# Moving one chunk's scores, its weighting and its normalisation ahead of weight roundings in the front of an mLSTM + FFN kernel

## The chip, the cores and the metric

The kernel runs on one core of a Trainium2 chip. The metric is the device time of one execution in microseconds. Before the change the median of three runs is 489.75 us (489.66 to 490.23).

## What is computed

Two stages follow each other. The first is an mLSTM cell over `q`, `k`, `v` of shape (4, 8, 768, 40) with an input, a forget and an output gate:

```python
for t in range(S):
    m_new = max(f[t] + m, i[t])
    f_stab, i_stab = exp(f[t] + m - m_new), exp(i[t] - m_new)
    C = f_stab * C + i_stab * outer(v[t], k[t])
    n = f_stab * n + i_stab * k[t]
    y[t] = sigmoid(o[t]) * (C @ q[t]) / max(abs(n @ q[t]), 1)
```

Its output is turned into `x` of shape (3072, 320), and the second stage is a feed-forward block with a squared ReLU:

```python
h = maximum(x @ w_in, 0)      # w_in: 320 x 2048
out = (h * h) @ w_out         # w_out: 2048 x 320
```

The weights arrive as 64-bit numbers and are made into f32 on the chip.

## The kernel before

**Tiles.** The sequence is cut into 24 chunks of 128 tokens (batch 0 has chunks 0 to 5). For a chunk `s` the recurrence is computed in its parallel form: `transposes` turns k and q, `scores` multiplies them (L595), `weigh` makes the decay weights W on ScalarE (ACT) from a log-decay tile `A_bc`, after `mask` on GpSimd (POOL) has cut it to the causal part, and `weighted` multiplies scores and W into P on VectorE (DVE, L609). `rows_begin` and `rows_end` (L700) then multiply old state, P and k with the values on TensorE (PE); between their two halves stands a DVE instruction of one element, the marker (L737), that reads the first half's result and writes a spare place that the second half's operand tile holds, so that PE's second half waits for it. `normalise` (L910 to L921) makes the chunk's rows of `x_sb`, and `turn_rows` (L951, L953) turns them into `xT`.

**Groups.** Two chunks make a group of 256 tokens. The first feed-forward product of a group is done in four parts of 512 columns. `ffn1_main` (L977) multiplies the first 256 rows of `w_in` in two K halves `a` of 128 rows, `ffn1_rest` (L988) adds the last 64 rows. `relu_half` (L1001) moves the result from PSUM to SBUF, `square_half` (L1007) squares it.

**Weight roundings.** The 64-bit weights come in 18 pieces. `Rounding.fetch` (L206) issues the load of a piece on SyncE's queue (SP), `words` (L216, L218) does two ACT passes, `join` three DVE passes (L227, L231, L232) and one addition on POOL (L236), and then fetches another piece into the buffer that it has freed. Pieces 0 to 9 are `w_in`: 0, 1 and 2 serve FFN1 part 0; 3 and 4 part 1; 5, 6 and 7 part 2; 8 and 9 part 3. Raw pieces 3, 7 and 11 lie in a tile that is lent (`lent_t`), the others in three buffers in turn.

**Order.** Nothing reorders the program: each engine and each DMA queue runs its instructions in the order in which the Python code issues them. The front is a hand-written order: chunks 0 and 1, then a loop over eight steps `u`, two for each of the chunks 2 to 5. An even step has scores, `weighted` and the next chunk's `weigh`; an odd step has the products with values, the next transposes and a normalisation. Every step has one part of FFN1 and one or more roundings, up to the count in `NEXT`. `idle(n)` (L1224) issues n matmuls of zeros whose result nobody reads. After the front, from about 86 us on, the other 18 chunks run beside the second product of the groups, with PE busy nearly throughout.

The change touches the loop nest of `ffn1_main` and steps `u` = 0, 1 and 2.

## Time and profile before

| | before |
|---|---|
| median of the runs | 489.75 us (489.66 to 490.23) |
| profiled execution | 489.91 us, span 488.2 us, mean granted clock 0.992 |
| PE busy | 476.6 us (98%) |
| weight loads busy | 444.6 us (91%) |
| DVE, ACT, POOL busy | 344.1, 244.0, 224.9 us |
| DMA | 69.93 MB, 143 GB/s mean |

The page tells busy time by engine, the span in forty slices, the queues, the chain of work that ended last, and groups of instructions. PE is busy 98% of the span, so its idle time (11.6 us in all) and the clock that it is granted are what a change in the front can work on. The front is about 86 us long; in it DMA is near its full share, and every engine works for several purposes in turn, so a wait there is best read from the timeline of each queue.

### The profile page before, as it was taken

What the parts mean: (1) busy time and instruction counts of PE and PEld (TensorE: products, weight loads), DVE (VectorE), ACT (ScalarE), POOL (GpSimd) and SP (SyncE); (2) the same over time, 40 slices, a digit from 0 to 9 for tenths busy, and PEclk for the clock granted to TensorE, in tenths of its full rate; (3) what the DMA queues carried; (4) which work ended last, traced back from release to release, by engine and by line L of the source; (5) the groups of instructions that cost most, each with busy time, mean ns of one, the idle gap of its engine ahead of it and who ended that gap; (6) DMA issues with size and microseconds to landing.
All of it is one profiled execution on the core that took longest, in us unless ns stands there. A gap on an engine that the chain in (4) does not pass through costs nothing.

```text
span 488.2 us, 15700 instructions
## 1 busy us (share of the span) xinstructions
PE 476.6 (98%) x6389; PEld 444.6 (91%) x6389; DVE 344.1 (70%) x725; ACT 244.0 (50%) x534; POOL 224.9 (46%) x337
## 2 busy tenths in 40 slices
PE   9989999999898999999999999999999999999997
PEld 5877788779798999999999999999999999999997
DVE  7959768888886974775876975965965957635441
ACT  4697897644641651652752751653653651514300
POOL 5454545567881876826746836734833111020000
PEclk9988999999999999999999999999999999999999
DMA  8999998779997698677677686696773322200000
GB/s 174 209 253 265 259 202 209 201 144 230 194 190 108 165 169 164 164 155 155 149 149 153 159 165 145 155 155 128 156 144 87 93 58 82 55 15 15 1 28 27
DMA packets 192839, 69.93 MB, mean 143 GB/s; under 512 B 158144, under 2 KB 181504, under 8 KB 192768
## 3 DMA queue, kind: packets, MB, share of 16 engines
q1 hardware_dynamic: 157424, 56.39, 51.7%
q0 software_dynamic: 6080, 10.16, 9.4%
q10 hardware_dynamic: 29264, 2.39, 4.7%
q8 instruction: 50, 0.82, 0.7%
q14 instruction: 21, 0.17, 0.1%
HBM read 55.69 MB, written 18.92 MB: 153 GB/s over the span
## 4 chain that ended last, share of the span: by engine, by line
PE 77%; DMA 10%; SPq 6%; DVE 3%; ACT 1%; issue 1%; POOL 0%; DVEq 0%; ACTq 0%; POOLq 0%
PE h_ps L1061 32%; PE h_ps L1140 22%; PE h_ps L1173 7%; PE h_ps L977 5%; DMA kqT<-kq_rows 3%; PE numT L823 3%; DMA kq<-in_q_dram 2%; PE numT L801 2%; SPq L399 2%; PE tp L587 1%; PE h_ps L988 1%; DMA xT<-x_rows 1%; PE numT L835 1%; DMA raw<-in_moe_w_in_dram 1%; SPq L206 1%
## 5 line engine op out<-in xcount | busy, mean ns | idle before, releaser
L1061 PE MATMUL h_ps<-T,S 128*128 128x160 f32 x352 | 51.6, 300 | 0.7 <-DVE S L1056 0.7
L1061 PEld LDWEIGHTS h_ps<-T,S 128*128 128x128 f32 x352 | 48.9, 190 | 1.1 <-PE h_ps L1061 0.9
L1061 PE MATMUL h_ps<-w_out,g 128*128 128x160 f32 x336 | 48.8, 302 | 0.0
L1061 PEld LDWEIGHTS h_ps<-w_out,g 128*128 128x128 f32 x336 | 46.2, 190 | 1.1 <-issue 0.5
L1077 DVE TENSOR_TENSOR y_sb<-y_sb,h_ps 128x160 f32<-128x160 f32 x44 | 14.0, 318 | 45.2 <-PE h_ps L1061 45.1
L1154 ACT COPY r_sb<-h_ps 128x512 f32<-128x512 f32 x20 | 11.7, 584 | 65.5 <-PE h_ps L1140 54.0
L1140 PE MATMUL h_ps<-xT,w_in 128*128 128x128 f32 x320 | 43.2, 278 | 0.0
L1140 PE MATMUL h_ps<-lent_t,w_in 128*128 128x128 f32 x320 | 42.3, 275 | 0.0
L1173 PE MATMUL h_ps<-xT,w_in 64*64 64x128 f32 x960 | 39.5, 272 | 1.8 <-DVE r_sb L1156 1.8
L1132 POOL TENSOR_TENSOR lent_t<-xT 128x128 f32<-128x128 f32 (+1 forms) x18 | 10.3, 592 | 66.7 <-DVE xT L943 50.6
L1140 PEld LDWEIGHTS h_ps<-xT,w_in 128*128 128x128 f32 x320 | 39.2, 192 | 1.6 <-issue 1.2
L375 POOL DMA_DIRECT2D va<-in_v_dram x64 | 39.3, 630 | 0.3 <-issue 0.3
L1140 PE MATMUL h_ps<-lent_t 128*128 128x128 f32 x320 | 39.1, 275 | 0.0
L1140 PEld LDWEIGHTS h_ps<-lent_t,w_in 128*128 128x128 f32 x320 | 39.0, 192 | 0.0
L1140 PEld LDWEIGHTS h_ps<-lent_t 128*128 128x128 f32 x320 | 37.3, 192 | 0.2 <-issue 0.2
L1173 PEld LDWEIGHTS h_ps<-xT,w_in 64*64 64x64 f32 x960 | 35.1, 133 | 2.6 <-DVE r_sb L1156 2.1
L510 ACT ACTIVATE A_bc<-A_bc,b_R 128x64 f32<-128x64 f32 (+1 forms) x128 | 35.6, 362 | 0.1
L1191 ACT ACTIVATE g<-h_ps 128x512 f32<-128x512 f32 x12 | 7.2, 597 | 53.6 <-PE h_ps L1140 36.3
L479 POOL TENSOR_SCALAR_AFFINE_SELECT A_bc<-A_bc 64x512 f32<-64x512 f32 x32 | 25.7, 802 | 17.0 <-ACT kq L497 15.8
L977 PE MATMUL h_ps<-xT,w_in 128*128 128x256 f32 x128 | 31.6, 402 | 0.0
L858 DVE STREAM_TRANSPOSE tn<-numT 128x256 f32<-128x256 f32 x36 | 14.0, 425 | 23.4 <-PE numT L801 15.5
L531 POOL TENSOR_TENSOR vw<-va,A_bc 128x328 f32<-128x328 f32 x13 | 11.5, 886 | 39.6 <-ACT A_bc L510 39.6
(231 smaller groups left out, 1213.5 us busy)
## 6 DMA issues: line engine op xcount, KB each, us to landing
A_bc<-a_slots SPq DMA_DIRECT2D x32, 256.0 KB, 4.3
kq<-num_rows SPq DMA_DIRECT2D x80, 64.0 KB, 3.1
num_rows<-tn SPq DMA_DIRECT2D x18, 256.0 KB, 2.4
raw<-in_moe_w_out_dram SPq DMA_DIRECT2D x7, 640.0 KB, 4.8
og<-in_o_gate_dram SPq DMA_DIRECT2D x24, 160.0 KB, 5.1
x_rows<-x_sb SPq DMA_DIRECT2D x20, 192.0 KB, 2.6
xT<-x_rows SPq DMA_DIRECT2D x80, 48.0 KB, 2.6
out_dram<-y_sb SPq DMA_DIRECT2D x23, 160.0 KB, 2.5
```

Source lines behind the costliest of these rows:

```text
L375: eng.dma_start(dst[HALVES[n], PR * (1 - late_keys) : PR * (2 - late_keys)], src[HALVES[late_keys], PR * m : PR * (m + 1)],)
L479: nc.gpsimd.affine_select(part, part, compare_op=ALU.is_ge, fill=-1e30, base=0, pattern=[[0, PR], [0, 2], [1, DP]], channel_multiplier=-1,)
L510: nc.scalar.activation(A[0][:, x, to], A[0][:, x, to], AF.Exp, bias=b_R[:, b, c, own, x : x + 1],)
L531: nc.gpsimd.tensor_tensor(d["vw"][:].rearrange("p (own x) d -> p own x d", own=2), d["va"][:].rearrange("p (own x) d -> p own x d", own=2) ...
L823: nc.tensor.matmul(d["numT"][m][DP * e : DP * e + wide, i, t0:], lhsT=va_w[s % NKQ][keys, at * D1 : at * D1 + wide], rhs=rhs, start=(s % N ...
L858: nc.vector.transpose(to[:, 2 * m : 2 * m + 2], d["numT"][m].rearrange("p c t -> p (c t)"))
L977: nc.tensor.matmul(hs[i][:, n, :], lhsT=w_in[:, a, fb * P : (fb + 1) * P], rhs=xT[:, :, a, :], start=(n == 0 and a == 0), stop=False,)
L1061: nc.tensor.matmul(to, lhsT=lhsT[:, p], rhs=rhs[:, p, :], start=(start and p == 0), stop=(p == NPAIR - 1), skip_group_check=True,)
L1077: add = lambda to, a, b: nc.vector.tensor_tensor(to, a, b, op=ALU.add)
L1140: nc.tensor.matmul(to[:, n, :], lhsT=lhsT[:, 4 * q + n, :], rhs=rhs, start=(start and n == 0), stop=True, skip_group_check=True,)
L1154: nc.scalar.copy(m1[:], X[:])
L1173: nc.tensor.matmul(to[cols, n, :], lhsT=w_in2[rows, 4 * q + n, cols], rhs=rhs, start=(start and n == 0), stop=True, skip_group_check=True,)
```

## The change

In `ffn1_main` the loop over the two K halves goes outside, so that all four column blocks are multiplied with the first 128 rows of the weights before any is multiplied with the second 128.

In the front, join 3 (which stood ahead of the loop) and join 4 (in step 0) each move behind something:

- step 0: the scores of chunk 2 go between FFN1 part 0's main and rest; the mask of chunk 3 follows at once, then P of chunk 2, and only then join 3. Step 0 ends with four joins done instead of five.
- step 1: join 4 stands between the two halves of chunk 2's products, behind the marker. The load of `A_bc` for chunk 4 is thereby issued ahead of raw piece 8. The normalisation of chunk 2 goes ahead of join 5, and the tanh of chunk 3's output gate behind the copies of the turned k and q.
- step 2: `idle(3)` becomes `idle(1)`.

Nothing is computed otherwise than before.

```diff
-        for i in range(2):
-            for n in range(2):
-                fb = 4 * pp + 2 * n + i
-                for a in range(2):
+        for a in range(2):
+            for i in range(2):
+                for n in range(2):
+                    fb = 4 * pp + 2 * n + i
                     nc.tensor.matmul(
                         hs[i][:, n, :], lhsT=w_in[:, a, fb * P : (fb + 1) * P], rhs=xT[:, :, a, :],
                         start=(n == 0 and a == 0), stop=False,
...
     weigh(2, masked=True)
     decay_old(2)
     rounding.words()
-    rounding.join()
-    NEXT = (5, 8, 10, 11, 12, 13, 14, 16)
+    NEXT = (4, 8, 10, 11, 12, 13, 14, 16)
...
             if u == 0:
-                ffn1(0, 0)
+                ffn1_main(0, 0)
                 scores(2)
+                ffn1_rest(0, 0, st["half"][0])
+                mask(3)
             else:
                 if u == 2:
-                    idle(3)
+                    idle(1)
...
             weighted(s)
             if u == 0:
-                mask(s + 1)
-                rounding.step()
+                rounding.join()
+                rounding.words()
+                rounding.words()
...
             if u == 1:
                 half_tanh(2)
-                half_tanh(3)
...
                 (rows_begin if s < X_SQ else attend_begin)(s)
+                if u == 1:
+                    rounding.join()
                 copies = transposes(s + 1, (True, True))
                 (rows_end if s < X_SQ else attend_end)(s)
...
+            if u == 1:
+                normalise(s)
             if u != 3:
                 rounding.join(fetch=u < 7)
             if u == 1:
                 load(4)
                 values(s + 1)
-            if s < X_SQ:
+            elif s < X_SQ:
                 normalise(s)
...
             copies()
+            if u == 1:
+                half_tanh(3)
             rounding.words()
             ffn1(u // 4, u % 4)
```

## The prediction

> **What bounds the kernel.** I read the page's first two parts, then the waits of TensorE (PE), the windows around the one dip of its clock, the chain, and last the queues' timelines from 20 to 60 us, where the change lies.

> ```profile
> PE 476.6 (98%) x6389; PEld 444.6 (91%) x6389; DVE 344.1 (70%) x725; ACT 244.0 (50%) x534; POOL 224.9 (46%) x337
> ...
> PEclk9988999999999999999999999999999999999999
> ...
> PE numT L700 <- DVE g_c L609: 0.7, 1, 0.7
> PE tp L555 <- DMA kq<-in_q_dram: 0.7, 1, 0.7
> ...
> 29.90:33.31 3.41, 2.48 (x80) 1.94 (x76) 3.31 (x6) 2.56 (x7) 2.51 (x2) 1.00 1.01 229
> 33.31:36.73 3.42, 2.95 (x45) 2.54 (x46) 1.13 (x4) 3.42 (x11) 1.26 (x1) 0.50 0.69 122
> 36.73:40.14 3.41, 3.41 (x9) 2.69 (x9) 3.31 (x9) 2.66 (x6) 1.98 (x3) 0.50 0.98 228
> 40.14:43.56 3.42, 3.42 (x20) 2.24 (x20) 3.25 (x8) 1.82 (x4) 1.02 (x2) 1.00 1.00 362
> ...
> 132.30:135.72 3.42, 2.16 (x94) 2.01 (x98) 2.98 (x6) 3.00 (x5) 1.49 (x3) 1.00 1.07 245
> ...
> 23.31 10.43 DMA kq<-in_q_dram
> 33.73 0.04 issue
> 33.78 1.12 PE tp L555 x4
> ...
> 42.95 0.76 PE idle L1224 x3
> ```

> PE is the bound, so only three things in the front can be won: two gaps (0.73 us until P of chunk 2, 0.67 us until q of chunk 3 lands), the filler L1224 (0.76 us), and the half clock from 33.31 to 40.14. In the windows the columns behind the length are busy us of PE, its weight loads, DVE, ACT, POOL, then granted clock, DMA share and GB/s. The clock falls at the end of a stretch that holds both gaps and only small matmuls, and stays low for 6.83 us. The chain says why PE starts again at 33.78: q's DMA, issued at 23.31 and 10.43 us under way.

> ```profile
> 41.16 0.68 ACT L216 ACTIVATE mag<-lent_t 128x512 f32<-128x512 f32 x1 [1.42 <-POOL vw L537]
> 42.98 1.08 ACT L1001 ACTIVATE g<-h_ps 128x512 f32<-128x512 f32 x2 [0.57 <-PE h_ps L988]
> 44.35 0.48 ACT L956 COPY xT<-tp 128x384 f32<-128x384 f32 x1 [0.28 <-PE tp L953]
> ...
> 52.12 0.16 DVE L737 TENSOR_SCALAR kq<-numT 1x1 f32<-1x1 f32 x1
> 52.36 0.33 PEld L700 LDWEIGHTS numT<-vw,kq 64*64 64x64 f32 x16 [0.17 <-DVE kq L737]
> ```

> Here ACT is seen to be the second bound: its second rounding of piece 7 starts at 41.16, when that piece's DMA lands (issued 35.65, 5.4 us), and everything after it is in one file, up to DVE's marker L737, for which PE waits at 52.36.

> **Part by part.** The profiled execution took 489.91 us (span 488.2, 1.7 around it); the median of the runs is 489.75. Differences below are worked out in the span and then taken from the median.

> 1. *Scores of chunk 2 ahead of the 64-row rest of FFN1.* The same 16 records of L595 (1.06 us) and 8 of L988 (1.14) swap places, so PE reaches 30.0 us as before. P (L609, 1.29 for both halves) needs the scores at 29.1 instead of 30.06, and as DVE no longer does a rounding (28.35 to 30.25) before it, it runs 29.1 to 30.4 instead of 30.28 to 31.57. The 0.73 us gap goes.

> 2. *What is late next.* PE does L700 (some 1.2 us) and the four k transposes from 30.0 and is done at about 31.9 (k lands at 22.77 + 8.6 = 31.4) instead of 33.11. Then it waits for q. Nothing ahead of q on SP is moved, so q lands at 33.73 as before, and the gap there is 1.8 us instead of 0.67. Gain of parts 1 and 2 together: 0.

> 3. *The clock.* The stretch 29.90 to 33.31 holds the same work after the change: 72 records of L700 and 4 transposes, with at most 0.1 us of L988 in place of the scores' end, and 1.4 us idle at its end instead of 0.96 in two pieces. PE's busy time alone does not decide: the stretch 132.30 to 135.72 has less (2.16) and keeps the clock. Weighing every record by the part of the array it fills (rows x columns / 128 x 128) times its columns streamed, twice for f32, I get 2254 for the stretch that loses the clock and 2860 for the one at 132.30 that keeps it. After the change I get 2254 to 2480. The next stretch (q's transposes, 40 records, two of FFN1) is unchanged too. So the clock falls at 33.31 and returns at 40.14: 0. Bounds: -3.4 us (half of 6.83) if it stays up and nothing else binds; +1.7 if a third stretch of 3.41 us is lost.

> [...]

> 4. *P, mask and marker ahead of roundings.* POOL's mask of chunk 3 (1.28) goes ahead of the rounding's addition; A_bc lands at 21.99 + 8.5 = 30.5, so it runs to 31.8 instead of 32.94, and ACT's exponentials (2.45) start after the relu at 32.1 instead of 32.97. Nobody waits for them: DVE needs them at 46. Join 3 moves to 30.4-32.3 (1.9), the marker to 32.3, join 4 (2.45) to 32.5-35.0, its addition to 36.3 on POOL. PE's rest of chunk 2 starts at 34.83 after q's transposes, as before. FFN1 part 1 starts at 36.28 and needs piece 4 only for its second half, 3.6 us later at half clock. Cost 0, hidden under q's DMA; uncovered, the addition would cost 0.1.

> 5. *K halves.* 16 records of L977 per part (3.72) in another order, none added. The second piece is needed 1.9 us later, the second bank 0.9 us earlier; the relus that free it (1.08) end 0.8 us or more ahead, part 3 excepted (point 8). From 0.3 gain (piece 9 is added until 53.51, part 3 starts at 53.20) to 0.2 loss; taken: 0.

> 6. *Normalisation ahead of join 5.* x_sb is ready at about 40 instead of 42.30. Join 5 (1.85) ends at 41.7 instead of 39.05; POOL's addition and vw of chunk 3 move from 39.20-41.16 to 41.7-43.7. Part 2 needs piece 5 at 44.8: hidden by 1.8 us.

> 7. *Filler.* Two of three L1224 go: 0.76 x 2/3 = 0.51 us. PE reaches the turned rows at 43.2 instead of 43.71, with x_sb long ready. Of this, ACT passes on less: its relu starts at 42.98 as before (PE's L988 ends at 42.95), the copy of xT at 44.06 instead of 44.35. From there piece 8, the exponentials, piece 9, join 9 and the marker follow on ACT and DVE without a break, so marker and PE stand at 52.07 instead of 52.36. Gain 0.29 us. Between 0.29 and 0.51 I take 0.3, since PE does wait for that marker.

> 8. *SP's queue.* A_bc of chunk 4 goes ahead of raw 8 (0.8 us each way, landing at 42.4 and 43.4, needed from 44). Raw 9 needs the buffer that join 5 frees, so it is issued at 41.75 instead of 39.12, and k, q and v of chunk 4 and raw 10 stand behind it. Issued at once after it, q lands at about 48 (was 39.98 + 7.2 = 47.2), and PE transposes it at 51. Raw 10 lands near 51 instead of 50.1, and ACT wants it at 50.5: piece 10 and the relu of part 2 may be 0.5 to 1 us late, which part 3 feels by 0 to 0.2 and ACT's idle 1.55 us before 58.02 takes up. SP stood idle 46.74-49.26, so it has caught up by raw 12. Cost 0 to 0.2; taken 0, as rows with idle follow.

> From 53 us PE, DVE, ACT and SP are all 0.3 us earlier, so the later chains move as a whole. Sum: 0 + 0 + 0 - 0.3, so 489.75 - 0.3 = **489.5 us** rounded.

> **Rivals.**

> *The clock stays up.* If the stretch counts a little more of L988, or stands otherwise against the program. Then q's transposes take 0.5 instead of 1.1, L700 0.85 instead of 1.45, and FFN1 part 1 ends at 39.9 instead of 42.95: 3 us. But ACT is then in piece 7 until 42.4 (41.16 + 1.25), so relu, xT copy and the file behind them come at most 44.72 - 43.7 = 1.0 us earlier, and PE waits at the marker. Time: 489.75 - 1.0 = 488.7; lower still, to 487.2, only if that file is shorter than I read. Against it: the sums of point 3; the runs (489.66 to 490.23) show no second state in which the clock is kept. [...] Chance 0.18.

> *Slower: a second fall of the clock at 132.* The stretch from 132.30 counts 2860, and PE waits 1.75 us for DVE in front of it. If the work there comes 0.2 us later against the stretch, I count 2696, 0.5 later 2450: at some point it falls, and dense L1061 behind it (136.18 on) runs at half clock for 3.41 us, 1.7 us lost. It needs the front to be late by 0.2 us or more, as when raw 9's wait on join 5 holds SP longer than point 8 says (q of chunk 4 past 51, or piece 10 past 52). 489.75 + 0.3 + 1.7 = 491.7. A front that is 0.3 us early moves away from it (3344), and one that is 1.0 early comes into the stretch before it (2640 from 129.90). Chance 0.27, with other late pieces (x_sb, piece 5) in it at +1 to +2.

> *The change does nothing:* q's DMA and ACT's file take up all, the filler too. 489.75; part of the likeliest case's own range, 489.1 to 490.0.

> **The numbers.** Likeliest 0.55 (489.5), clock kept 0.18 (488.7), slower 0.27 (491.7 and around). 0.2% is 0.98 us, about what a measurement of this kernel can tell from no change. Faster than 488.77: the lower half of the clock case, 0.15, and 0.05 for misjudged ACT: 0.20. Slower than 490.73: 0.27, and 0.03 for the tail of the likeliest: 0.30. Same: 0.50. The range takes in both rivals and leaves a tenth on either side: 488.1 to 491.8.

> **What would show it.** Right: PE's wait for L609 gone, its wait for q 1.6 us or more, clock 0.50 from about 33.3 for 6.8 us, FFN1 part 1 still ending near 42.9, marker L737 near 51.9, SP's raw at 41.7. Wrong: q landing well before 33.7; clock 1.00 from 33 to 40; PE waiting for x_sb, piece 5 or q of chunk 4; a second 0.50 anywhere behind 100 us.

## The result, and the profile after

The kernel before took 489.32 us (median of 22 executions beside the new kernel, 486.14 to 493.51), the changed one 491.67 us (22, 487.79 to 495.25). The ratio is 1.0042, with a 95% interval of 1.0022 to 1.0062: by this measurement the change costs about 2 us, where 0.3 us of gain was forecast. Medians take in all executions; ratios, and the means further down, leave out those more than 1.5% above the fastest of the same kernel. Single executions of either kernel differ by several us, so a profile of one execution cannot be set against a profile of another and the difference called the change.

The profiled execution of the changed kernel took 492.29 us (span 490.6). From its page, the busy line, the granted clock and the queue that brings instructions:

```profile
PE 474.4 (97%) x6386; PEld 442.9 (90%) x6387; DVE 340.8 (69%) x725; ACT 243.7 (50%) x534; POOL 224.7 (46%) x337
...
PEclk9999999999999999999999999999999999999999
...
q8 instruction: 50, 0.82, 0.7%
```

The half clock in the front, which the prediction took as a fixed cost of 6.83 us at half speed, is not there. TensorE's waits from 0 to 480 us show what stands in the way instead (engine, line waited for, us in total, times, longest):

```profile
PE h_ps L977 <- POOL w_in L236: 2.3, 3, 1.2
...
PE numT L700 <- DVE kq L737: 1.3, 1, 1.3
PE numT L801 <- DVE A_bc L609: 1.3, 1, 1.3
PE numT L835 <- issue: 1.2, 1, 1.2
...
```

Three things are to be seen. The wait for P (L609 ahead of L700) is gone, and there is no long wait for q: q of chunk 3 landed at 31.39 us, not at 33.73. FFN1's parts now wait 2.3 us for POOL's additions, and TensorE still waits 1.3 us at the marker L737. And a new line says that TensorE stood 1.2 us at L835, at 229.3 to 230.6 us, for nothing that the profile shows ("issue"); below this is called the stand. It lies 146 us behind the last matmul of the lines that the diff touches (L977, until 83.5 us).

The clock did fall, elsewhere. The windows of the changed kernel around that place (length, busy us and count of PE, its weight loads, DVE, ACT, POOL, granted clock, DMA share, GB/s):

```profile
130.43:133.84 3.41, 1.94 (x75) 1.71 (x76) 3.26 (x6) 3.25 (x5) 1.75 (x3) 1.00 0.99 249
133.84:137.25 3.41, 3.41 (x47) 3.08 (x48) 1.93 (x5) 1.23 (x4) 1.91 (x3) 0.50 0.82 139
```

Set against the profile of before, part 3 of FFN1 (L977) starts 0.75 us earlier (52.45 against 53.20), and the end comes 2.4 us later. On the way 1.2 us go at L835. Some 2 us more go between 305 and 318 us, where DVE waits for two round trips through DRAM, as its waits in that window show:

```profile
DVE dm L890 <- DMA kq<-num_rows: 1.5, 1, 1.5
...
DVE xT L943 <- DMA xT<-x_rows: 0.8, 1, 0.8
```

None of the other sixteen profiles of this study has a loss of this size there (L1077 is a DVE addition that runs 100 times, and the times of its starts serve as marks along the kernel; from the 41st to the 55th start it is 62.9 to 63.8 us in them and 65.2 in this one), so these 2 us belong to that execution and not to the change.

### The profile page after: what moved, and what is told of

The parts are those of the page before. It is cut to its first block, busy times and chain, and to the rows that moved or that the text cites. A ratio compares the mean times of both kernels' runs of the same rounds, so it can differ in the third digit from the quotient of the medians.

```text
span 490.6 us, 15695 instructions
## 1 busy us (share of the span) xinstructions
PE 474.4 (97%) x6386; PEld 442.9 (90%) x6387; DVE 340.8 (69%) x725; ACT 243.7 (50%) x534; POOL 224.7 (46%) x337
## 3 DMA queue, kind: packets, MB, share of 16 engines
q10 hardware_dynamic: 29264, 2.39, 4.5%
## 5 line engine op out<-in xcount | busy, mean ns | idle before, releaser
L1061 PE MATMUL h_ps<-T,S 128*128 128x160 f32 x352 | 51.7, 300 | 2.1 <-DVE S L1056 1.7
L1061 PEld LDWEIGHTS h_ps<-T,S 128*128 128x128 f32 x352 | 48.8, 190 | 2.8 <-PE h_ps L1061 2.2
L1061 PE MATMUL h_ps<-w_out,g 128*128 128x160 f32 x336 | 49.7, 305 | 0.0
L1061 PEld LDWEIGHTS h_ps<-w_out,g 128*128 128x128 f32 x336 | 47.2, 193 | 1.3 <-issue 0.7
L1077 DVE TENSOR_TENSOR y_sb<-y_sb,h_ps 128x160 f32<-128x160 f32 x44 | 14.0, 318 | 46.4 <-PE h_ps L1061 46.4
L1140 PE MATMUL h_ps<-lent_t,w_in 128*128 128x128 f32 x320 | 42.4, 275 | 0.1
L1132 POOL TENSOR_TENSOR lent_t<-xT 128x128 f32<-128x128 f32 (+1 forms) x18 | 11.3, 645 | 66.6 <-DVE xT L943 48.0
L1173 PE MATMUL h_ps<-xT,w_in 64*64 64x128 f32 x960 | 39.5, 272 | 1.2 <-DVE r_sb L1156 1.2
L1173 PEld LDWEIGHTS h_ps<-xT,w_in 64*64 64x64 f32 x960 | 35.1, 133 | 1.9 <-DVE r_sb L1156 1.5
L977 PE MATMUL h_ps<-xT,w_in 128*128 128x256 f32 x128 | 30.2, 386 | 2.3 <-POOL w_in L236 2.3
```

Of the source, the lines that this page charges most:

```text
L977: nc.tensor.matmul(hs[i][:, n, :], lhsT=w_in[:, a, fb * P : (fb + 1) * P], rhs=xT[:, :, a, :], start=(n == 0 and a == 0), stop=False,)
L1061: nc.tensor.matmul(to, lhsT=lhsT[:, p], rhs=rhs[:, p, :], start=(start and p == 0), stop=(p == NPAIR - 1), skip_group_check=True,)
L1077: add = lambda to, a, b: nc.vector.tensor_tensor(to, a, b, op=ALU.add)
L1132: sub = lambda to, a, b: eng.tensor_tensor(to, a, b, op=ALU.subtract)
L1140: nc.tensor.matmul(to[:, n, :], lhsT=lhsT[:, 4 * q + n, :], rhs=rhs, start=(start and n == 0), stop=True, skip_group_check=True,)
L1173: nc.tensor.matmul(to[cols, n, :], lhsT=w_in2[rows, 4 * q + n, cols], rhs=rhs, start=(start and n == 0), stop=True, skip_group_check=True,)
```

## The experiments

Four theories were set against each other. *Fetch*: the change takes out two fillers with their weight loads, so everything behind stands four TensorE instructions earlier in the instruction stream, and a block of instructions arrives too late at 229 us. *Clock*: the stretches of 3.41 us after which the clock is halved lie otherwise against the program in each execution, so each meets other thin ones. *Front*: the new order of the front delays later chains. *Chance*: there is no difference. Every kernel is compared with the kernel before on the same chip at the same time, since chips differed by about 3 us (before's median was 486.70 us on one and 489.88 on another). The column "mean" below is the mean of 11 or 12 executions (after: 21) minus the mean of before's that ran beside them, with its standard error. The times inside the kernel come from one profiled execution each; "fetch asked to TensorE's next" is the time from the start of the transfer on the instruction queue until TensorE goes on behind the stand.

| kernel | PE instr. against before | stand at L835, us | fetch asked to TensorE's next, us | 27th to 29th L1077, us | mean against before, us |
|---|---|---|---|---|---|
| before (on record) | 0 | none | - | 23.7 | - |
| after (on record) | -4 | 1.23 | 2.27 | 25.1 | +1.8 ± 0.6 |
| before_again | 0 | none | - | 23.5 | -0.1 ± 0.6 |
| after_again | -4 | 1.19 | 2.19 | 25.0 | +1.5 ± 0.7 |
| after_idle3 | 0 | none | - | 24.2 | -0.7 ± 0.4 |
| before_idle1 | -4 | 0.96 | 2.35 | 24.8 | +1.6 ± 0.6 |
| after_pad2 | 0 | none | - | 23.5 | -0.1 ± 0.6 |
| before_less2 | -4 | 1.03 | 2.20 | 24.9 | +1.2 ± 0.8 |
| after_raw8 | -4 | 1.42 | 2.39 | 26.8 | +0.5 ± 0.7 |
| after_raw8_pad2 | 0 | none | - | 24.3 | +0.3 ± 0.7 |
| after_pad1 | -2 | 1.17 | 2.26 | 25.0 | +0.1 ± 0.6 |
| after_noK_pad2 | 0 | none | - | 23.6 | +0.4 ± 0.7 |
| after_late2 | 0 behind 129 us | none | - | 23.5 | +0.6 ± 0.7 |
| after_third | -4 | 0.90 | 2.35 | 24.7 | +1.6 ± 0.7 |
| after_fill | +14 behind 149 us | none | - | 24.2 | -0.8 ± 0.5 |
| before_fill | +18 behind 149 us | none | - | 24.4 | -0.9 ± 0.5 |
| before_fill_b | +18 behind 149 us | none | - | 24.4 | -0.2 ± 0.5 |

### The same kernels again, and the filler alone

before_again and after_again are the two kernels unchanged. The other two exchange the filler alone:

```diff
# after_idle3, against after
-                    idle(1)
+                    idle(3)
# before_idle1, against before
-                    idle(3)
+                    idle(1)
```

> The kernel before, unchanged, beside itself, to see how its own executions differ. Clock theory (the windows in which the clock is halved run free of the program, so every execution meets the thin stretches differently): the granted clock of its executions takes several values between 0.990 and 1.000, the profile's dip of 0.50 is not at 33.3 us again or has another length, and the longer executions have the lower clock. Rival (the dip at 33.3 belongs to the program): all executions show 0.992 and the dip is at 33.3 for 6.8 us again. Time 489.3, ratio 1.000 within 0.002 under both.

> The kernel after, unchanged, on the same chip as the other three. If the loss belongs to the change: 1.004, 491.5 us, as on record. If it was the chip or the hour: within 0.002 of 1. Fetch theory (four TensorE instructions fewer move the places where the next block of instructions is fetched): TensorE again stands 1.2 us for nothing but issue at L835 near 230.5. Clock theory: that stand may be gone, but the dip near 134 is back in about half of the executions, and those are 1 us longer or more. Front gain of 0.75 us at part 3 (PE L977 at 52.45 instead of 53.20) under all, unless the dip falls into the front.

> The kernel after with the three fillers of before (idle(3) instead of idle(1)), nothing else: TensorE again has as many instructions as before, and 0.51 us of filler that should hide before the marker L737. Fetch theory: no stand at L835 near 230, the loss of the change goes or shrinks by 1.2 us or more: 489 to 490.3, ratio 0.998 to 1.002. Front theory (the order of the front makes later chains of DMA late): as after, 491.5, ratio 1.004. Clock theory: no change in the mean against after beyond 0.5 us.

> The kernel before with one filler instead of three, nothing else. My recorded step 7 alone: 0.3 us less, 489.0. Fetch theory: the front gains 0.3, TensorE stands 1.2 us at L835 near 230, and the kernel is 1 to 2 us slower than before: 490.3 to 491.3, ratio 1.002 to 1.004. Front theory and clock theory: ratio within 0.002 of 1.

Measured: before_again 489.56 us (ratio 0.9994, 0.9963 to 1.0025), after_again 491.79 (1.0027, 0.9992 to 1.0061), after_idle3 488.69 (0.9993, 0.9964 to 1.0021), before_idle1 491.08 (1.0026, 0.9994 to 1.0057). Each interval by itself reaches 1, but the order is what the fetch theory asks for, and the traces show it directly: the stand is in the two kernels with one filler and not in the two with three. In the front the filler alone gained nothing, where 0.3 us was expected: with one filler before_idle1 reaches part 3 of FFN1 at 51.86 us, and the four profiles of before's order with three fillers and the clock up reach it at 51.82 to 52.07.

before_again settles the clock of the front: unchanged code, and this time no half clock at 33 us but one at 133.89, where the changed kernel had it too. Its windows:

```profile
130.48:133.89 3.41, 1.84 (x75) 1.68 (x74) 3.30 (x6) 3.36 (x6) 1.21 (x3) 1.00 0.96 254
133.89:137.30 3.41, 3.41 (x47) 3.08 (x48) 1.87 (x5) 1.07 (x4) 1.99 (x3) 0.50 1.08 147
```

So the fall at 133.8 us is no effect of the change, and neither is its absence in the front.

### The number of instructions, moved to another place

If the number counts and not the place, two fillers more or fewer at the very start, where TensorE waits for DVE anyway (0.43 us in before_again, 0.59 in after_again), must switch the stand at 229 us off and on.

```diff
# after_pad2 (against after); after_pad1 has idle(13)
-    idle(12)
+    idle(14)
# before_less2 (against before)
-    idle(12)
+    idle(10)
```

> The kernel after, with two more fillers at the very start (idle(12) becomes idle(14), where TensorE stands 0.43 to 0.59 us for DVE anyway), so that TensorE has as many instructions ahead of everything later as the kernel before, while the changed front stays as it is. Fetch theory: no stand at L835 near 229 (1.0 to 1.2 us in the three kernels with one filler), the stretch from 225 to 249 takes 23.5 to 24.2 us instead of 25.0, and the median falls from 491.7 to 490.4 or lower. Rival (it was the filler's place, not the number, that mattered: PE reaches the turned rows 0.5 us too early): the stand stays and the median stays at 491.7.

> The kernel before with two fillers fewer at the very start (idle(12) becomes idle(10)), nothing else. The front at 42 us keeps its three fillers. Fetch theory: TensorE stands 1.0 to 1.3 us for issue at L835 near 229 though nothing that the diff of the change touches is touched; median 490.7 to 491.2, ratio 1.002 to 1.004. Rival (place, not number): no stand there, 489.6, ratio 1.000.

> The kernel after with one more filler at the very start (idle(13)): two TensorE instructions fewer than before instead of four. Fetch theory: either the stand at L835 near 229 is there with 2.2 to 2.4 us from the fetch's start to TensorE's next instruction, and then the time is as after (491.0 to 491.7), or the fetch is asked for before the wait of L587, the stand is gone and the time is as with fourteen (489.2). A stand of half the length would speak against the theory, since a request is either ahead of the wait or behind it.

Measured: after_pad2 489.24 us beside 489.16 of before (1.0000, 0.9966 to 1.0035), before_less2 490.71 (1.0017, 0.9981 to 1.0054). TensorE's waits between 224 and 235 us in before_less2, whose text differs from before in nothing but the start:

```profile
PE numT L835 <- issue: 1.0, 1, 1.0
```

And its waits between 200 and 260 us in after_pad2, which has the whole changed front and no stand:

```profile
PE numT L835 <- DVE kq L792: 2.5, 1, 2.5
...
```

The rival (the filler's place) is out: the stand follows the number. after_pad1 has it at -2 already, at the same place of TensorE's stream (the 5826th record; the 5824th to 5826th in all seven profiles that have it, and a trace can lack a record or two: after's page counts three matmuls fewer than before's, 6386 and 6389, where two went). Its time is a miss, though: 487.50 us beside 487.31, ratio 0.9998 (0.9968 to 1.0028), where the stand in its trace should have cost about 1.2 us. With a standard error of 0.6 us this is 1.7 errors off; one kernel with 12 executions cannot tell 1.2 us from nothing reliably. after_raw8, below, is a second such case: a stand of 1.42 us, and a mean of +0.5 ± 0.7.

Why a fetch: the instruction queue (q8) carries 50 transfers of 16,384 bytes beside 12,955 recorded TensorE instructions in before; between the starts of its first (14.32 us) and its last (468.90 us) TensorE goes through 12,520 of them, 255.5 a transfer on the mean and 93 to 441 from one start to the next. In the ten profiles without a stand the transfer that matters starts when TensorE is at its 5560th to 5632nd record; in the seven with one it starts at the 5718th to 5750th, with 80 to 110 instructions left to the place of the stand, and TensorE goes on 2.2 to 2.4 us after that start, whatever else differs. In the kernel before it starts at 227.24 us, 0.06 us after the first weight load of L835; in the changed one at 228.30, 0.1 us after the first weight load of the next line that waits, L587, and TensorE's records break off at 229.3. That TensorE stands for this transfer is a reading of these times: the profile itself puts the 0.90 to 1.42 us down to "issue". That a request goes out only when the wait ahead of it has been passed was a reading of these two profiles. It does not fit all seven with a stand: in before_less2, before_idle1 and after_third the transfer starts 0.01 to 0.29 us ahead of L587's first weight load. What sets off the request stays open.

### The order on SP's queue

The prediction gave 0 to 0.2 us for A_bc of chunk 4 ahead of raw 8 and for raw 9 behind join 5. Put back was the first:

```diff
-            if u < 7:
+            if 1 < u < 7:
                 load_A(s + 2)
...
                 if u == 1:
                     rounding.join()
+                    load_A(4)
```

after_raw8_pad2 has idle(14) at the start as well.

> The kernel after with the order on SP's queue put back: raw 8 ahead of A_bc of chunk 4 (A_bc moves behind join 4). ACT's file theory (the front of the change is 0.45 us later than that of before where the clock stays up in both, because ACT waits 0.86 us for raw 8): raw 8 lands near 43.2, ACT's wait for it is 0.1 or less, marker L737 near 50.6 instead of 51.3, first L1015 at 85.0 instead of 85.7. The stand at L835 stays (1.2 us), so the median is 491.0, 0.7 less than after. Rival (the front does not matter, it is given back by 130 us): L1015 earlier, but the median as after, 491.7, and the starts of L1077 from 175 on as in after.

> Both edits together: raw 8 ahead of A_bc, and two more fillers at the very start. If both theories hold and add up: front 0.6 earlier than after, no stand at L835, median 489.7 minus what the kernel before loses in its front to the halved clock in some executions: 488.5 to 489.5, ratio 0.997 to 1.000. If the stretch from 86 to 130 takes the front's gain back: 490.0 to 490.4.

Measured: after_raw8 489.17 us beside 489.16 (1.0002, 0.9966 to 1.0038), after_raw8_pad2 488.70 (1.0010, 0.9975 to 1.0045; the medians say less and the ratio more than 1, which shows the scatter). The front did not get earlier: marker L737 stands at 51.76 and 51.31 against 51.28 in after_again and after_pad2, so this expectation failed. ACT's waits from 36 to 54 us, first in after_again, then in after_raw8:

```profile
...
ACT lent_t L216 <- DMA raw<-in_moe_w_in_dram: 0.9, 1, 0.9
ACT mag L216 <- DMA raw<-in_moe_w_out_dram: 0.2, 1, 0.2
```

```profile
...
ACT mag L216 <- DMA raw<-in_moe_w_out_dram: 1.1, 1, 1.1
...
```

The wait for raw 8 (0.9) is gone, and ACT ends its first pass of piece 9, which the marker's chain needs, 0.48 us earlier (49.12 against 49.60). The wait for raw 10, which has grown from 0.2 to 1.1 us, stands behind that pass on ACT and cannot hold the marker. What holds it is DVE, which runs join 9 (L227, L231, L232) and then the marker, and POOL beside it. From the timelines of after_again (two lines) and after_raw8 (three):

```profile
49.63 0.43 DVE L227 TENSOR_SCALAR mag<-mag 128x512 f32<-128x512 f32 x1 [1.44 <-ACT mag L216]
...
51.28 0.15 DVE L737 TENSOR_SCALAR kq<-numT 1x1 f32<-1x1 f32 x1
```

```profile
48.98 1.27 POOL L236 TENSOR_TENSOR w_in<-lent_t 128x512 int32<-128x512 int32 x1 [1.62 <-DVE lent_t L232]
49.16 1.38 DVE L227 TENSOR_SCALAR mag<-mag 128x512 f32<-128x512 f32 x1 [0.32 <-ACT mag L216]
...
51.76 0.16 DVE L737 TENSOR_SCALAR kq<-numT 1x1 f32<-1x1 f32 x1
```

In after_raw8 L227 starts earlier, but it starts while POOL's addition for piece 8 runs, takes 1.38 us instead of 0.43 and ends 0.29 us behind that addition. The same is seen in 13 of the 17 profiles: wherever this L227 starts during the addition, it ends 0.28 or 0.29 us after it. So the marker follows DVE's file, its instructions from 36 us on in their order: in nine of the eleven profiles of the changed order the marker comes 12.80 to 12.82 us after the start of join 5, whenever raw 8 and raw 10 land. In the other two, after and after_again, ACT is the later one and adds 0.2 us. More than that A_bc ahead of raw 8 is not seen to cost in these traces.

What the changed order does to DVE's file is seen at join 6, first in before, then in after:

```profile
42.68 0.43 DVE L231 TENSOR_SCALAR mag<-mag 128x512 int32<-128x512 int32 x1
43.14 0.69 DVE L232 SCALAR_TENSOR_TENSOR mag<-raw,mag 128x512 int32<-128x512 int32 x1
```

```profile
40.13 1.33 POOL L236 TENSOR_TENSOR w_in<-lent_t 128x512 int32<-128x512 int32 x1 [2.54 <-DVE lent_t L232]
40.36 1.38 DVE L231 TENSOR_SCALAR mag<-mag 128x512 int32<-128x512 int32 x1
41.42 0.92 POOL L537 TENSOR_TENSOR vw<-va,g_c 128x328 f32<-128x328 f32 x1
41.78 1.11 DVE L232 SCALAR_TENSOR_TENSOR mag<-raw,mag 128x512 int32<-128x512 int32 x1
```

With the normalisation ahead of join 5, POOL's addition for piece 5 and vw run beside join 6 and no longer beside the normalisation. Join 6 takes 2.9 us instead of 1.5 in every profile, the normalisation 2.4 instead of 3.3 and join 5 1.5 instead of 1.8. Beside before's join 6 POOL does nothing (41.16 to 43.97 us). In sum DVE's file from the first instruction behind L754 to P of chunk 3 (L609) is 0.2 us longer: 9.19 to 9.30 us in the eleven profiles of the changed order, 9.06 to 9.09 in the six of before's.

In after_raw8 the clock fell behind the stand (the windows give 1.98 busy us of 3.40 from 227.20, then 0.50), which makes its stretch 26.8 us: this half clock follows the stand in one of the seven traces that have one.

### FFN1's parts without K halves

```diff
# after_noK_pad2: after with idle(14) at the start, and in ffn1_main
-        for a in range(2):
-            for i in range(2):
-                for n in range(2):
-                    fb = 4 * pp + 2 * n + i
+        for i in range(2):
+            for n in range(2):
+                fb = 4 * pp + 2 * n + i
+                for a in range(2):
```

> The kernel after with two more fillers at the very start (no stand at L835) and FFN1's parts in the old order instead of K halves. My step 5 (the order is worth nothing): first L1015 at 85.7 as in the kernels with K halves, median 489.2 like fourteen fillers alone. Rival (K halves help, since the second piece of each part is late): TensorE's waits for POOL's additions grow from 0.7 to 1.5 us to 2 us and more, but marker L737, which waits for ACT, stays at 51.3, so even then L1015 moves by 0.3 us or less.

Measured: 488.21 us beside 487.31 (1.0003, 0.9972 to 1.0035), L1015 at 85.72 us (85.66 in after_pad2), part 3 at 52.39 (52.33). TensorE's waits from 20 to 56 us, without K halves:

```profile
PE h_ps L977 <- POOL w_in L236: 3.7, 3, 2.2
...
```

and in after_pad2, which has them:

```profile
PE numT L700 <- DVE kq L737: 1.1, 1, 1.1
PE h_ps L977 <- ACT g L1001: 1.1, 1, 1.1
...
PE h_ps L977 <- POOL w_in L236: 0.2, 1, 0.2
...
```

The two lists end at the same place: 3.7 us for POOL and none at the marker, or 0.2 us for POOL and 1.1 at the marker, with part 3 within 0.06 us. K halves do take away the wait that they are for, and it comes back at the marker, because DVE's file has not moved (the marker comes 12.80 us after the start of join 5 without K halves, 12.81 with them).

### Filling the thin stretches

```diff
+    def fill(n):
+        X = st["f1"][0]
+        for _ in range(n):
+            nc.tensor.matmul(X[:], lhsT=zeros[...], rhs=zeros[...], start=False, stop=True, ...)
...
+            if n == 9:
+                idle(3)
             if not joined(s):
                 do(attend_begin, s)
...
             if fast:
+                if n == 13:
+                    fill(6)
                 ffn1_rows(g, 0, True)
```

> The kernel after with nine fillers in two places where TensorE waits for DVE: three ahead of the attention at 129 us (it waits 0.95 us for A_bc there), six that add zero times zero to an open sum ahead of L1173 at 149 us (it waits 1.95 us for r_sb). Clock theory (a stretch of 3.41 us whose weighed work is under about 2500 is followed by one at half clock): no dip at 130 to 137 and none at 148 to 156 in this execution or most others, the stretches there weigh 3500 or more; 36 instructions of difference aside, each dip avoided is worth 1.3 to 2.5 us. Fetch theory: eighteen TensorE instructions more ahead of 229 move the fetch ahead of L587's wait, so that the stand at L835 is gone too. Both: median 488.0 to 489.0. Rival (dips are not due to thin stretches): dips as often as in the others, the fillers cost what they last beyond the waits, 0 to 0.5 us, median 489.2 to 492.

> The kernel before with the same nine fillers. Clock theory: dips only in the front at 29 to 40 us, if at all; median 1 us or more below before: 488.0 to 488.6, ratio 0.996 to 0.998. Rival: ratio 1.000 to 1.001. If after_fill and before_fill agree within 0.7 us, what is left of the change without its stand and without the dips is nothing that can be measured.

> The kernel before with nine fillers at 129 and 149 us a second time, on this chip. Clock theory: again 0.7 to 1.4 us below before. Rival (the first value was scatter): 0 within 0.6 us.

Measured: after_fill 486.60 us and before_fill 485.89 beside 487.31 (both 0.9983; 0.9954 to 1.0012 and 0.9955 to 1.0011), before_fill_b 486.54 beside 486.70 (1.0008, 0.9982 to 1.0035). At the two places the clock stays up in all three profiles: after_fill's windows there (from an execution whose clock fell in the front instead) show it:

```profile
129.20:132.60 3.40, 3.40 (x99) 2.82 (x101) 3.06 (x6) 3.40 (x6) 1.64 (x4) 1.00 1.10 208
148.20:151.60 3.40, 3.10 (x57) 1.90 (x60) 2.22 (x4) 0.00 (x0) 0.00 (x0) 1.00 0.65 130
```

No trace of the three with fillers has a half clock between 130 and 160 us, and seven of the fourteen others have. A gain in time is not shown: the means are -0.8, -0.9 and -0.2 us, every interval has 1 in it, and the second measurement of before_fill went with the rival (0 within 0.6 us), not with the 0.7 to 1.4 us that the clock theory asked for. No version of this study is shown to beat the kernel before.

### With and without the stand, on one chip

```diff
# after_late2, against after: two fillers at 129 us, none added at the start
+            if n == 9:
+                idle(2)
             if not joined(s):
                 do(attend_begin, s)
```

> The kernel after with two more fillers at 129 us (ahead of the attention, where TensorE waits for DVE), so that the first 129 us have the instructions of after and everything behind them stands where it stood in before. Fetch theory: no stand at L835 near 229, stretch from 225 to 249 (25th to 29th L1077) 23.5 to 24.3 us, mean 1.2 us below after in the same call: 0 to +0.5 against before. Rival (the start-up matters: a front that begins with fewer fillers loses the rest): stand gone but the mean stays 1.5 us above before.

> The kernel after, unchanged, beside after_late2. Fetch theory: the stand is there, and the mean is 1.0 to 1.6 us above before. If it is 2 us or more, something of the change beyond the stand costs time; if it is under 0.8, the first measurement was high by its scatter.

(The stretch meant is that from the 27th to the 29th start of L1077, as in the table.) Measured: after_third 488.56 us beside 486.70 (1.0041, 1.0008 to 1.0075), after_late2 487.41 (0.9998, 0.9963 to 1.0034). The first 129 us have the same instructions; the difference of the two means is 1.0 us (standard error 1.0), the stretch differs by 1.2 (24.7 and 23.5), and the stand in after_third is 0.90 us. The means, +1.6 for after_third (expected 1.0 to 1.6) and +0.6 for after_late2 (expected 0 to 0.5), go with the fetch theory but are too few to prove it by themselves.

Taken together: the 91 executions in the seven rows with the stand (after three times) have a mean of +1.24 us against before, standard error 0.27; the 69 in the six rows without stand and without the nine fillers have +0.06 ± 0.27; the 57 in the five among these that carry the changed front, +0.08 ± 0.29. The difference, 1.2 ± 0.3 us, has the size of the stand in the traces (0.90 to 1.42 us). What the rest of the change is worth cannot be told from zero. On this reading the 2 us of the first measurement are the stand, and the rest is scatter.

## Why the prediction was wrong, step by step

Steps 1 and 2 (the scores' gap goes, 1.8 us of waiting for q come in its place): the first half was right, L609 no longer holds TensorE. The second was wrong in one assumption: q's landing at 33.73 us was read as a property of the kernel. In after's execution q landed at 31.39, and in before_again, which has the old order, q landed at 31.30 and TensorE does not wait for it at all. FFN1's part 1 started at 33.78 us instead of 36.28.

Steps 4 and 6 (mask, P, marker and normalisation at no cost): step 6 saw that POOL's addition for piece 5 and vw would move behind join 5, but not that DVE's join 6 would then run beside them and take 2.9 us instead of 1.5. With what the normalisation and join 5 gain, that makes DVE's file 0.2 us longer. What step 4 said of FFN1, that it needs no rounding early, held at half clock only; at full clock part 1 comes 2.5 us sooner and waits for POOL's additions (2.3 us in all in after). That is hidden, as the K-halves experiment shows, by the marker.

Step 5 (K halves, 0): right, for a reason that was only half seen. They save up to 3.5 us of waiting for POOL and give it back at the marker and its neighbours.

Step 7 (filler, -0.3): this is the step that failed, in size and in sign. It had the 0.3 us reach the marker through ACT, which the prediction took for the second bound. What the marker waits for is DVE with POOL beside it, in the profile of before too: there ACT's first pass of piece 9 ends at 50.27 us, but L227 ends at 50.90, 0.28 us after POOL's addition, so 0.29 us gained on ACT would be lost there. DVE's file already runs when the fillers come (42.89 us in before), and from the start of join 6 to the marker it takes 9.90 to 9.92 us in before, before_again, before_idle1 and before_fill, with three fillers or with one. The marker is at 50.81 us with one filler (before_idle1) and at 50.77 to 51.02 with three and the clock up: the gain is nothing. And the step counted the two fillers as time only. They are also four instructions of the stream, and taking these out, in the changed front or in a front otherwise untouched, puts 0.9 to 1.4 us of stand at 229 us.

Step 8 (SP's queue, 0 to 0.2, taken 0): the size was about right, the path was not. The step had raw 9 and raw 10 late and part 3 waiting for them. Raw 9 is issued at 39.98 instead of 37.83 us (after_again and before_again) and raw 10 lands at 50.32 instead of 49.85, but neither is what the marker, and part 3 behind it, waits for. What SP's order costs is the 0.2 us by which ACT, late with raw 8, is behind DVE in after and after_again. With the clock up in both, part 3 starts at 51.82 to 52.07 us in the five such profiles with before's front, and at 52.07 to 52.81 in the nine with the changed front and one filler at that place: 0.5 us later between the middles (51.92 and 52.38). Of this, 0.2 us is DVE's longer file; the rest is a later start of that file and, in two profiles, ACT, and differs from one profile to the next. By the end of the kernel this 0.5 us cannot be told from zero (+0.08 ± 0.29).

The rivals. "The clock stays up" described the front of the profiled execution well (0.75 us early against the 1.0 given, and a wait at the marker as it said), but before's own front keeps its clock in five of six profiles too. "A second fall of the clock at 132" gave 491.7 us, which is what came out, by a mechanism that is not the cause: the fall at 133.84 is there, costs 1.2 us or more (the first to the sixth start of L1077 take 12.3 to 12.7 us in the three profiles with this fall and at most 11.1 in those that keep the clock there; 1.7 was forecast), and is in the unchanged kernel as well. A forecast that meets the number by another road is not confirmed.

What stays open: what sets off the request for instructions, so for another edit it can't be said beforehand whether the count will hurt; and whether the 0.5 us of the front is given back or hidden in the scatter.

## What to carry to other kernels

Before a difference between two profiles is explained, take a second profile of the unchanged kernel: here a half clock of 6.83 us at 33.31 us and the landing of a transfer at 33.73 us, both read as fixed, were different in the next execution (3.41 us at 133.89, and 31.30 us). One or two fillers fewer among 12,955 recorded TensorE instructions went with a stand of 0.90 to 1.42 us at 229 us, in the changed kernel 146 us behind the lines of the edit; look for idle time put down to "issue" far behind an edit, and test it by adding the same number of harmless instructions somewhere else. Removing a wait (P 0.7 us, POOL's additions up to 3.5, raw 8 0.9) was worth nothing here while the engine that ends last in that stage, DVE with its joins up to the marker and POOL's additions beside them, stayed as it was (12.80 to 12.82 us from join 5 to the marker in nine of eleven profiles). To find that engine, take the chain backwards from the instruction that is waited for: a wait on another engine in the same stretch, as ACT's for raw 8 (0.9 us) and raw 10 (0.2 to 1.1), need not lie on it.

## What the runs showed of the hardware that was not expected

- TensorE stood 0.90 to 1.42 us for "issue" in all seven profiles of kernels that had two or four TensorE instructions fewer, always at the 5824th to 5826th record, 2.2 to 2.4 us after the 16 KB transfer had started, though that transfer itself took 0.93 us (after).
- A DVE pass over 128 x 512 elements (L227) took 0.43 us alone and 0.53 to 1.45 us when it started during POOL's addition of the same size (1.27 us); it then ended 0.28 or 0.29 us after that addition, in all 13 profiles in which join 9 met it.
- In before's own order a stand for issue of 1.10 to 1.35 us occurs at 41.2 us (weight load of L951) in every profile whose front kept its clock. It is in none with the changed front; where it is, the marker hides it.
- The place of the half clock changed between executions of the same code (33.3 us for 6.83 us, 133.9 us for 3.41 us, or none ahead of 480 us), worth 1.2 us or more at 133.9 us and, at 33.3 us in before's front, 1.1 us or more at part 3 of FFN1. A part of the spread of single times (3 to 9 us between the fastest and the slowest) stays without an explanation: executions at clock 1.00 took from 487.8 to 491.8 us.
